# Where the first x tiles are transposed, and on which queue w1's first pieces travel: a silu MLP on one core

## The chip, the cores and the metric

One core of a Trainium2 chip runs the whole program. The time is device microseconds of one execution; the time before is the median of three runs.

## The reference

```python
# x: 1 x 2048 x 640, w1: 640 x 1728, w2: 1728 x 640, all bf16
h = jnp.einsum("bsd,df->bsf", x, w1)
h = jax.nn.silu(h)
out = jnp.einsum("bsf,fd->bsd", h, w2)
```

## The kernel before, in words

The 2048 rows of x are four row chunks of 512 (`sc` 0 to 3). The contraction of the first product, 640, is five tiles of 128 (`dt` 0 to 4). The 1728 columns of w1 are thirteen column tiles of 128 (`ft` 0 to 12) and a tail of 64.

TensorE needs x transposed, with the contraction on the partitions: `xT_sb[:, dt, rows]`. For chunks 1 to 3 all five tiles come by DMA transpose, straight from x in memory (`transpose_x`, L152, on SP's queue). For chunk 0 the tiles come in two ways: tiles 0 to 2 are loaded as they lie (`load_x0`, L144, into `x0_sb`), transposed on TensorE by four 128x128 transposes each (`transpose_x0`, L181, against an identity), and copied from PSUM to `xT_sb` by VectorE (tiles 0 and 2, L185) or ScalarE (tile 1, L187); tiles 3 and 4 come by one DMA transpose each.

w1's columns 0 to 767 (column tiles 0 to 5) come as one load of 192 KB for each contraction tile (`w1_0` to `w1_4`, L148), the rest in two loads for all five contraction tiles: `w1_a` (column tiles 6 to 9, 640 KB) and `w1_b` (column tiles 10 to 12 and the tail, 560 KB).

TensorE's order is written by hand. After a few matmuls on constants (L171) and the transposes of tile 0, `column_group` (L262) computes column tiles 0 to 5 of chunk 0 at once in six PSUM banks: the outer loop is over the contraction tiles, the inner one over the six column tiles, so each contraction tile is used for six matmuls as soon as it is there. After the second matmul of tile `dt` it calls `transpose_next(dt + 1)`, which puts the transposes of the next tile into TensorE's stream if that tile is transposed there, and otherwise only notes the DMA to wait for. The first matmul of tile `dt` waits for that x tile and for `w1_dt`. Then `unit` (L220) computes column tiles 6 to 12 of chunk 0, each with five matmuls; the first of them waits for `w1_a`. Chunk 1 has a `column_group` and units again, chunks 2 and 3 have units alone, and two `tail_unit`s (L230) compute the last 64 columns of two chunks each. A column tile's silu is a sigmoid on ScalarE (L204) and a product on VectorE (L207).

The second product (L325) follows, with copies out of PSUM (L336, L338) and the stores.

SP issues, in this order: half of x's tile 0, `w1_0`, `w1_1`, `w1_2`, the transpose of tile 3, `w1_4`, the transpose of tile 4, `w1_a`, `w1_b`, then the fifteen transposes of chunks 1 to 3 (the first of which wait for `w1_a`), with w2's loads after ten of them. ScalarE issues: the other half of tile 0, tile 1 (`x0_c`), tile 2 (`x0_d`), `w1_3`; then comes its activation table load and a small activation (L162), and only then its copy of tile 1. Waits are semaphore waits that `Plan` puts ahead of an instruction for the operations it depends on.

Of the kernel before, what the change touches and what calls it, by code (L numbers as in the profile page):

```python
# [20 lines left out]
class Plan:  # L21
# [9 lines left out]
    def add(self, eng, emit, deps=(), group=None):  # L31
        op = Op(eng, emit, [d for d in deps if d is not None], group)
        self.ops.append(op)
        return op
# [40 lines left out]
def bass_standalone__dense_activation_silu__prompt_kernel(  # L75
# [9 lines left out]
    xf = x.flatten_outer_dims()  # L85
# [3 lines left out]
    P = 128  # L89
    H = P // 2  # L90
    SCH = 512
    DT = D // P
# [5 lines left out]
    JB = SCH // P  # L98
# [4 lines left out]
    with ExitStack() as es:  # L103
        def sb(name, shape, dtype):
            return es.enter_context(nc.sbuf_tensor(name, shape, dtype))

        xT_sb = sb("xT_sb", [P, DT, S], bf16)
# [18 lines left out]
        bank_free = [[] for _ in range(NBANK)]  # L126
        turn = [0]

        def take_bank():
# [5 lines left out]
        FA = 6  # L135
        w1_cuts = [FA, 10, FT]
        id_a = add("pool", lambda e: e.memset(ident[:, :], 0.0))
        id_b = add("pool", lambda e: e.affine_select(
            out=ident[:, :], in_=ident[:, :], compare_op=ALU.not_equal, fill=1.0,
            base=0, pattern=[[-1, P]], channel_multiplier=1), [id_a])  # L140
        warm = add("dve", lambda e: e.memset(warm_sb[:, :], 0.0))

        def load_x0(eng, name, j0, j1, d0, d1):
            return add(eng, lambda e: e.dma_start(  # L144
                out=x0_sb[:, j0:j1, d0 * P:d1 * P], in_=x0_v[:, j0:j1, d0 * P:d1 * P]), group=name)

        def load_w1(eng, name, d0, d1, f0, f1, deps=()):
            return add(eng, lambda e: e.dma_start(  # L148
                out=w1_sb[:, d0:d1, f0:f1], in_=w1_v[:, d0:d1, f0:f1]), deps, group=name)

        def transpose_x(sc, dt, name, deps=()):
            return add("sp", lambda e: e.dma_start_transpose(  # L152
                out=xT_sb[:, dt, sc * SCH:(sc + 1) * SCH],
                in_=xf[sc * SCH:(sc + 1) * SCH, dt * P:(dt + 1) * P]), deps, group=name)

        x0_a = [load_x0("sp", "x0_a", 0, JB // 2, 0, 1), load_x0("act", "x0_b", JB // 2, JB, 0, 1)]
        w1_lo = [load_w1("sp", "w1_0", 0, 1, 0, FA * P)]
        x0_c = [load_x0("act", "x0_c", 0, JB, 1, 2), load_x0("act", "x0_d", 0, JB, 2, 3)]
        w1_lo += [load_w1("sp", f"w1_{dt}", dt, dt + 1, 0, FA * P) for dt in (1, 2)]
        x0_t = {3: transpose_x(0, 3, "x0_3")}  # L160
        w1_lo += [load_w1("act", "w1_3", 3, 4, 0, FA * P), load_w1("sp", "w1_4", 4, DT, 0, FA * P)]
        add("act", lambda e: e.activation(out=warm_sb[:, :], in_=warm_sb[:, :], func=ACT.Sigmoid), [warm])  # L162
        x0_t[4] = transpose_x(0, 4, "x0_4")
        w1_dma = [load_w1("sp", f"w1_{name}", 0, DT, w1_cuts[g] * P, min(w1_cuts[g + 1] * P, F))
                  for g, name in enumerate("ab")]

# [9 lines left out]
        def transpose_x0(dt, j0, j1, b):  # L176

            dst = ps[:, b, :].bitcast(bf16)[:, j0 * P:j1 * P]
            out = xT_sb[:, dt, j0 * P:j1 * P]
            for j in range(j0, j1):  # L180
                t = add("pe", lambda e, j=j: e.transpose(  # L181
                    dst[:, (j - j0) * P:(j - j0 + 1) * P], x0_sb[:, j, dt * P:(dt + 1) * P], ident[:, :]),
                    [x0_a[j // (JB // 2)], id_b] if dt == 0 else [x0_c[min(dt, 3) - 1]] + bank_free[b])
            if dt % 2 == 0:
                c = add("dve", lambda e: e.tensor_copy(out=out, in_=dst), [t])  # L185
            else:
                c = add("act", lambda e: e.copy(out=out, in_=dst), [t])  # L187
            bank_free[b] = [c]
            return c
# [49 lines left out]
        x_dma, x1_of, w2_dma = {}, [], []  # L239
        for sc in range(1, NSC):  # L240
            for dt in range(DT):
                x_dma[sc] = transpose_x(sc, dt, f"x1_{dt}" if sc == 1 else f"x{sc}", [w1_dma[-2]])
                if sc == 1:
                    x1_of.append(x_dma[sc])
            if sc == 2:
                half = FR // 2
                for a, z in ((0, half), (half, FR)):
                    w2_dma.append(add("sp", lambda e, a=a, z=z: e.dma_start(
                        out=w2_sb[:, a:z, :], in_=w2_v[:, a:z, :]), group="w2"))
                for hh in range(2):  # L250
                    w2_dma.append(add("sp", lambda e, hh=hh: e.dma_start(
                        out=w2_sb[hh * H:(hh + 1) * H, FR, :], in_=w2[FR * P:F, :]), group="w2"))
# [18 lines left out]
        def transpose_next(dt):  # L271
            if dt in x0_t:
                x0T.append(x0_t[dt])
            elif dt < DT:
                x0T.append(transpose_x0(dt, 0, JB, FA + dt % 2))

        half = [transpose_x0(0, k * JB // 2, (k + 1) * JB // 2, FA - 2 + k) for k in range(2)]
        x0T = [half[1]]
        warm_up([SCH, 2 * P])
# [121 lines left out]
```

## Time and profile before

| | us |
|---|---|
| median of three runs (lowest to highest) | 125.83 (125.35 to 126.18) |
| the profiled execution's own time | 126.35 |
| its span, first to last instruction | 124.9 |

The early transfers, with the time at which the issue starts and, by the view of DMA issues, the time from there to landing:

| transfer | KB | queue | issue starts, us | to landing, us |
|---|---|---|---|---|
| x tile 0, two halves | 64 each | SP, ScalarE | 0.73, 0.74 | 2.1, 2.3 |
| `w1_0` | 192 | SP | 1.25 | 2.8 |
| `x0_c` | 128 | ScalarE | 1.26 | 3.2 |
| `w1_1` | 192 | SP | 1.75 | 3.4 |
| `x0_d` | 128 | ScalarE | 1.79 | 4.3 |
| `w1_2` | 192 | SP | 2.21 | 4.5 |
| `w1_3` | 192 | ScalarE | 2.35 | 4.5 |
| transpose of tile 3 | 128 | SP | 2.69 | 4.6 |
| `w1_4` | 192 | SP | 3.94 | 4.0 |
| transpose of tile 4 | 128 | SP | 4.55 | 3.7 |
| `w1_a` | 640 | SP | 5.73 | 6.4 |
| `w1_b` | 560 | SP | 6.35 | 7.2 |

How to read the profile: PE is TensorE's matmul, PEld its weight load, which overlaps the matmul before it; DVE is VectorE, ACT ScalarE; SPq and ACTq are instructions by which SP and ScalarE issue DMAs. `w_sb` stands for the tiles of w1 and w2, `x_sb` for `x0_sb`, and L152 is line 152 of the kernel. In the chain of waits each piece is the work that ended last, in order of time. All transfers of one queue go to the same 16 DMA engines; a transfer has landed when the last of them is done.

### The profile page before, as it was taken

Reading aid. Unit: us, or ns where it says so; the run is one execution under the profiler, and the core shown is the slowest. Engines: PE = TensorE matmul, PEld = TensorE weight load, DVE = VectorE, ACT = ScalarE, POOL = GpSimd, SP = SyncE. Lnnn points to the kernel's source line nnn. Section 1 sums busy time; section 2 is a strip of 40 time slices with the busy share of each in tenths; the row PEclk is TensorE's granted clock in tenths of the full one; section 3 lists DMA queues with packets and bytes.
Section 4 is the critical chain, followed back from the end, with each engine's and each line's share of the span. In section 5 each row is a group of like instructions: output and inputs, shape, how many; then the busy total and the mean of one; then the engine's idle time right before and its main releaser. Section 6 shows DMA issues by size and latency. Waiting matters only on the chain.

```text
span 124.9 us, 2083 instructions
## 1 busy us (share of the span) xinstructions
PE 121.9 (98%) x894; PEld 57.2 (46%) x894; DVE 45.2 (36%) x71; ACT 38.9 (31%) x68; POOL 0.7 (1%) x6
## 2 busy tenths in 40 slices
PE   7999999999999999999999999999999999999992
PEld 2444444444444444444444444444444444445482
DVE  0111985069666666666673020202020120202022
ACT  0503953087555555555540010101010110101021
POOL 2000000000000000000000000000000000000000
PEclk9999999999999999999999999999999999999999
DMA  3996384559980000000000001114120201112434
GB/s 86 314 273 239 90 89 98 113 132 381 306 170 0 0 5 0 3 0 0 0 0 5 0 0 32 26 21 154 66 105 5 105 0 21 26 21 74 157 104 111
DMA packets 20185, 10.41 MB, mean 83 GB/s; under 512 B 14416, under 2 KB 20176, under 8 KB 20176
## 3 DMA queue, kind: packets, MB, share of 16 engines
q1 hardware_dynamic: 18416, 9.62, 28.8%
q10 hardware_dynamic: 1760, 0.66, 2.0%
q8 instruction: 7, 0.11, 0.4%
q14 instruction: 2, 0.02, 0.1%
HBM read 4.90 MB, written 2.62 MB: 60 GB/s over the span
## 4 chain that ended last, share of the span: by engine, by line
PE 98%; DVE 0%; issue 0%
PE ps L325 47%; PE ps L220 35%; PE ps L262 11%; PE ps L171 3%; PE ps L230 2%; PE ps L181 1%; DVE o_sb L336 0%
## 5 line engine op out<-in xcount | busy, mean ns | idle before, releaser
L325 PE MATMUL ps<-w_sb,hT_sb 64*128 64x512 bf16 (+2 forms) x486 | 47.3, 352 | 0.0
L207 DVE TENSOR_TENSOR hT_sb<-ps,sig_sb 128x512 bf16<-128x512 f32 (+1 forms) x56 | 37.1, 688 | 21.6 <-ACT sig_sb L204 21.5
L220 PE MATMUL ps<-xT_sb,w_sb 128*128 128x512 bf16 x200 | 43.5, 379 | 0.0
L204 ACT ACTIVATE sig_sb<-ps 128x512 bf16<-128x512 f32 x54 | 30.7, 605 | 27.9 <-PE ps L220 16.4
L325 PEld LDWEIGHTS ps<-w_sb,hT_sb 64*128 64x128 bf16 x486 | 23.5, 94 | 23.5
L220 PEld LDWEIGHTS ps<-xT_sb,w_sb 128*128 128x128 bf16 x200 | 19.5, 98 | 23.7 <-DMA w_sb<-in_w_dram 0.3
L336 DVE CAST o_sb<-ps 128x512 bf16<-128x512 f32 (+2 forms) x9 | 5.7, 632 | 37.6 <-PE ps L325 37.6
L338 ACT CAST o_sb<-ps 128x512 bf16<-128x512 f32 (+2 forms) x9 | 4.8, 539 | 38.5 <-PE ps L325 38.5
L262 PE MATMUL ps<-xT_sb,w_sb 128*128 128x512 bf16 x60 | 14.5, 395 | 0.0
L325 PE MATMUL ps<-hT_sb,w_sb 64*128 64x512 bf16 x108 | 12.3, 376 | 0.0
L262 PEld LDWEIGHTS ps<-xT_sb,w_sb 128*128 128x128 bf16 x60 | 5.9, 101 | 7.2 <-issue 0.5
L325 PEld LDWEIGHTS ps<-hT_sb,w_sb 64*128 64x128 bf16 x108 | 5.2, 94 | 6.5 <-issue 0.4
L336 DVE CAST oT_sb<-ps 128x512 bf16<-128x512 f32 x2 | 1.4, 692 | 11.7 <-PE ps L325 11.7
L338 ACT CAST oT_sb<-ps 128x512 bf16<-128x512 f32 x2 | 1.2, 587 | 13.6 <-PE ps L325 13.6
L171 PE MATMUL ps<-const-bfloat16-1.0 128*128 128x512 bf16 (+1 forms) x8 | 3.3, 572 | 0.8 <-PEq L386 0.8
L185 DVE COPY xT_sb<-ps 128x256 bf16<-128x256 bf16 (+1 forms) x3 | 0.9, 336 | 6.2 <-PE ps L181 6.2
L230 PE MATMUL ps<-xT_sb,w_sb 128*64 128x512 bf16 x20 | 2.3, 381 | 0.0
L162 ACT ACT_TABLE_LOAD x1 | 1.3, 1283 | 2.9 <-issue 2.9
L171 PEld LDWEIGHTS ps<-const-bfloat16-1.0 128*128 128x128 bf16 x8 | 1.0, 137 | 1.9 <-issue 1.9
L181 PEld LDWEIGHTS ps<-ident,x_sb 128*128 128x128 bf16 x12 | 1.3, 129 | 1.2 <-DMA x_sb<-in_x_dram 0.6
L181 PE MATMUL ps<-ident,x_sb 128*128 128x128 bf16 x12 | 1.7, 281 | 0.0
L230 PEld LDWEIGHTS ps<-xT_sb,w_sb 128*64 128x64 bf16 x20 | 1.0, 110 | 1.2 <-issue 0.4
(9 smaller groups left out, 1.8 us busy)
## 6 DMA issues: line engine op xcount, KB each, us to landing
out_dram<-o_sb SPq DMA_DIRECT2D x14, 160.0 KB, 1.9
w_sb<-in_w_dram SPq DMA_DIRECT2D x1, 1120.0 KB, 7.7
w_sb<-in_w_dram SPq DMA_DIRECT2D x1, 960.0 KB, 5.6
w_sb<-in_w_dram SPq DMA_DIRECT2D x4, 192.0 KB, 3.7
w_sb<-in_w_dram SPq DMA_DIRECT2D x1, 640.0 KB, 6.4
w_sb<-in_w_dram SPq DMA_DIRECT2D x1, 560.0 KB, 7.2
xT_sb<-in_x_dram SPq DMA_TRANSPOSE x17, 3.1
x_sb<-in_x_dram ACTq DMA_DIRECT2D x2, 128.0 KB, 3.7
```

The source lines that it names most:

```text
L162: add("act", lambda e: e.activation(out=warm_sb[:, :], in_=warm_sb[:, :], func=ACT.Sigmoid), [warm])
L171: add("pe", lambda e, n=n: e.matmul(ps[:, NBANK - 1, 0:n], lhsT=ones[:, 0:P], rhs=ones[:, 0:n], start=True, stop=True))
L181: t = add("pe", lambda e, j=j: e.transpose(dst[:, (j - j0) * P:(j - j0 + 1) * P], x0_sb[:, j, dt * P:(dt + 1) * P], ident[:, :]), [x0_a[j ...
L185: c = add("dve", lambda e: e.tensor_copy(out=out, in_=dst), [t])
L204: a = add("act", lambda e: e.activation(out=sig_sb[:, s, 0:n], in_=ps[:, b, 0:n], func=ACT.Sigmoid), [pe, sig_free[s]])
L207: v = add("dve", lambda e, rows=rows, ft=ft, cols=cols: e.tensor_tensor(out=hT_sb[rows, ft, cols], in0=ps[rows, b, 0:n], in1=sig_sb[rows, ...
L220: pe = add("pe", lambda e, dt=dt: e.matmul(ps[:, b, 0:n], lhsT=w1_sb[:, dt, ft * P:(ft + 1) * P], rhs=xT_sb[:, dt, cols], start=(dt == 0), ...
L230: pe = add("pe", lambda e, dt=dt, hh=hh: e.matmul(ps[hh * H:(hh + 1) * H, b, :], lhsT=w1_sb[:, dt, FR * P:F], rhs=xT_sb[:, dt, (sc + hh) * ...
L262: pe = add("pe", lambda e, dt=dt, ft=ft: e.matmul(ps[:, banks[ft], :], lhsT=w1_sb[:, dt, ft * P:(ft + 1) * P], rhs=xT_sb[:, dt, sc * SCH:( ...
L325: pe = add("pe", lambda e, b=b, n=n, lhsT=lhsT, rhs=rhs, ft=ft: e.matmul(ps[:, b, 0:n], lhsT=lhsT, rhs=rhs, start=(swap == 0 and ft == 0), ...
L336: ev = add("dve", lambda e, b=b, n=n, dst=dst: e.tensor_copy(out=dst, in_=ps[:, b, 0:n]), [pe])
L338: ev = add("act", lambda e, b=b, n=n, dst=dst: e.copy(out=dst, in_=ps[:, b, 0:n]), [pe])
```

## The change

x's tile 2 of chunk 0 is no longer loaded and transposed on TensorE, but comes by DMA transpose, and tiles 3 and 4 come in one DMA transpose of 256 columns. `w1_2`, `w1_3` and `w1_4` are issued by ScalarE. SP's order becomes: half of tile 0, `w1_0`, `w1_1`, the transpose of tile 2, the transpose of tiles 3 and 4, `w1_a`, `w1_b`, and the rest as before. ScalarE's becomes: half of tile 0, `x0_c`, `w1_2`, `w1_3`, `w1_4`, and then the table load. TensorE's stream loses the four transposes of tile 2, and VectorE's their copy. `transpose_x` takes ranges of rows and tiles; for chunks 1 to 3 it moves what it moved.

```diff
-        def transpose_x(sc, dt, name, deps=()):
+        def transpose_x(name, r0, r1, d0, d1, deps=()):
             return add("sp", lambda e: e.dma_start_transpose(
-                out=xT_sb[:, dt, sc * SCH:(sc + 1) * SCH],
-                in_=xf[sc * SCH:(sc + 1) * SCH, dt * P:(dt + 1) * P]), deps, group=name)
+                out=xT_sb[:, d0:d1, r0:r1], in_=xf[r0:r1, d0 * P:d1 * P]), deps, group=name)
...
-        x0_c = [load_x0("act", "x0_c", 0, JB, 1, 2), load_x0("act", "x0_d", 0, JB, 2, 3)]
-        w1_lo += [load_w1("sp", f"w1_{dt}", dt, dt + 1, 0, FA * P) for dt in (1, 2)]
-        x0_t = {3: transpose_x(0, 3, "x0_3")}
-        w1_lo += [load_w1("act", "w1_3", 3, 4, 0, FA * P), load_w1("sp", "w1_4", 4, DT, 0, FA * P)]
+        x0_c = load_x0("act", "x0_c", 0, JB, 1, 2)
+        w1_lo += [load_w1(("sp", "act")[dt > 1], f"w1_{dt}", dt, dt + 1, 0, FA * P) for dt in range(1, DT)]
         add("act", lambda e: e.activation(out=warm_sb[:, :], in_=warm_sb[:, :], func=ACT.Sigmoid), [warm])
-        x0_t[4] = transpose_x(0, 4, "x0_4")
+        x0_t = {2: transpose_x("x0_t2", 0, SCH, 2, 3), 3: transpose_x("x0_t3", 0, SCH, 3, DT)}
+        x0_t[4] = x0_t[3]
...
-                    [x0_a[j // (JB // 2)], id_b] if dt == 0 else [x0_c[min(dt, 3) - 1]] + bank_free[b])
+                    [x0_a[j // (JB // 2)], id_b] if dt == 0 else [x0_c] + bank_free[b])
...
-                x_dma[sc] = transpose_x(sc, dt, f"x1_{dt}" if sc == 1 else f"x{sc}", [w1_dma[-2]])
+                x_dma[sc] = transpose_x(
+                    f"x1_{dt}" if sc == 1 else f"x{sc}", sc * SCH, (sc + 1) * SCH, dt, dt + 1, [w1_dma[-2]])
```

## Prediction

> **What bounds the kernel now.** I read the page first: who is busy, and which chain ends last.
>
> ```profile
> PE 121.9 (98%) x894; PEld 57.2 (46%) x894; DVE 45.2 (36%) x71; ACT 38.9 (31%) x68; POOL 0.7 (1%) x6
> ...
> PE 98%; DVE 0%; issue 0%
> PE ps L325 47%; PE ps L220 35%; PE ps L262 11%; PE ps L171 3%; PE ps L230 2%; PE ps L181 1%; DVE o_sb L336 0%
> ```
>
> TensorE is the whole chain. So an edit of the opening can win only the TensorE work it takes out, and can lose whatever time it makes TensorE wait. Next the chain of waits in order of time (start, duration, what):
>
> ```profile
> 5.66 1.68 PE ps L262 x6
> 7.34 0.22 PE ps L181 x4
> 7.56 4.75 PE ps L262 x22
> 12.31 7.56 PE ps L220 x35
> ```
>
> The second row is the four transposes of tile 2, the only TensorE work that the change removes: 0.22 us. Matmuls go at 4.75 / 22 = 0.216 us each. Then TensorE's weight loads, with what ended the idle time before them, and SP's rows of the same stretch:
>
> ```profile
> 12.11 1.12 SPq L152 DMA_TRANSPOSE xT_sb<-in_x_dram  x1
> 12.14 0.33 PEld L220 LDWEIGHTS ps<-xT_sb,w_sb 128*128 128x128 bf16 x3 [0.32 <-DMA w_sb<-in_w_dram]
> ```
>
> The first matmul of column tile 6 starts exactly when w1_a lands (SP's transpose, which waits for the same load, starts at 12.11). Nearly no TensorE time is lost there, but nothing is in hand either. Last, the DMA side: busy time by stretch (the last two numbers are the 16 engines' share and GB/s), and the transfers of a late stretch:
>
> ```profile
> 6.30:8.30 2.00, 2.00 (x14) 1.05 (x13) 0.42 (x1) 0.00 (x0) 0.00 (x0) 1.00 1.06 230
> 8.30:10.20 1.90, 1.90 (x10) 0.85 (x9) 0.00 (x0) 0.00 (x0) 0.00 (x0) 1.00 1.02 355
> ```
>
> ```profile
> DMA packets 39, 0.03 MB, mean 23 GB/s; under 512 B 0, under 2 KB 39, under 8 KB 39
> ## 3 DMA queue, kind: packets, MB, share of 16 engines
> q1 hardware_dynamic: 39, 0.03, 6.7%
> ```
>
> The engines are full to 10.2 us. From 8.3 to 10.2 they move 1.9 x 355 = 675 KB, about all of w1_a (640 KB), which nevertheless lands at 5.73 + 6.4 = 12.1. The second view (11.8 to 13.3) says why: a share of 6.7% is one engine of sixteen, still working alone. One engine lags, and w1_a and w1_b land with it. I read w1_a as 10.5 without that lag (10.2, and some 0.3 from last packet to landing), so the lag is 1.6 us.
>
> **The change, part by part.** TensorE loses four transposes: -0.22 us from 7.18 on. VectorE's copy of tile 2 (0.42 us) goes too; VectorE then idles 3.9 us, so that is worth nothing. The 22 matmuls start at 7.18 in place of 7.40, so the needs become: tile 2 at 8.04, tile 3 at 9.34, tile 4 at 10.63, column tile 6 at 11.93.
>
> ScalarE's queue: x0_d goes, w1_2 and w1_4 come, one issue of 0.53 us more. The table load goes from 2.91 to 3.44 and the warm activation ends at 4.96 in place of 4.43. What is queued behind is the copy of tile 1, which starts at 5.70 when TensorE delivers: 0.74 us of cover, price nothing; if an issue took over 1.3 us, tile 1 would be late by the excess.
>
> SP's queue: after w1_1 comes tile 2's transpose at 2.21, issue 1.13 to 1.26 us by the undisturbed rows, 1.20 for the row in the same place; then the double one at 3.46. No row shows a double transpose. Low bound: one issue, 1.2, so w1_a goes out at 4.7 against 5.73. Middle: two singles, 2.4, w1_a at 5.9. High: twice the longest row (1.93, behind w2's loads), 3.9, w1_a at 7.4. I take between the first two, since the rows of the loaded opening are 1.13 and 1.20.
>
> DMA work: x0_d is 512 pieces of 256 bytes, a transposed tile moves the same bytes. A steady transpose costs 0.45 of the engines for its 1.3 us step, 0.59 us; the DMA records give 18 ns a piece for x0_d too, 512 x 18 / 16 = 0.58. So the swap is neutral. Bytes ahead of w1_a are unchanged, and the engines stay full, since ScalarE's three 192 KB loads are queued by 3.5 us. All of it should be done where it is done today: the last tile lands at 4.55 + 3.7 = 8.3 now.
>
> When each lands: the two queues seem to share the engines about evenly from 4 us. w1_1 (0.53 us of work, a quarter already done) is through at 4.8, tile 2 at 5.9, landing at 6.6 with 0.7 for the tail (tile 3 today: pieces done near 6.6, landed 2.69 + 4.6 = 7.3). w1_2 at 5.6, w1_3 at 6.8, w1_4 at 7.6; the double one at 8.4 to 8.9. Cover: tile 2 1.4 us, w1_2 2.4, w1_3 2.5, w1_4 3.0, tiles 3 and 4 0.4 to 0.9 (tile 3 has 2.2 today). The thin one is the double transpose: tile 3 now waits for both halves.
>
> A transpose of four 128x128 blocks lands 2.6 us after its issue when alone, and the next one follows in 1.3 us, so blocks overlap. The Trainium skill (VectorE: DVE Perf Modes, The three transpose paths) gives one 128x128 transpose 390 ns on TensorE and 1309 ns by DMA, which speaks against the swap; by that, an estimate, twelve DMA blocks in a row would end near 17.9. The trace does not agree: four blocks in 2.6 us are half of that, and they overlap. What the rule would mean here is rival E.
>
> w1_a: same bytes ahead, same lag: 12.1, bounds 10.5 (no lag) and 13.8 (lag once more, or issued 1.6 later). TensorE wants it at 11.93. At 12.1 the 0.22 that was saved is spent waiting. w1_b (13.6 against a need of 16.5) and the first tile of the next rows (14.7 against 19.9) are far from being next.
>
> Sum: -0.22, given back up to 0.2: 0 to -0.22, I take -0.05. Against the profiled execution of 126.35 (span 124.9, 1.4 around it) that is 126.3; the median of the runs is 0.5 lower, so the forecast is 125.83 - 0.05 = 125.8.
>
> **The rivals.**
> B, slower: the double transpose is dear behind a loaded queue. For: transposes behind loads took up to 7.5 us to land and 1.93 to issue (the w2 stretch), and no row shows a double. At 3.46 + 7.5 = 10.9 tile 3 is 1.6 late, net +1.4; at 3.9 of issue w1_a goes out 1.63 later and lands at 13.7, net +1.6. The two overlap. Price 126.1 to 127.6, as one number 127.4. It decides where the double lands after 9.56 (9.34 + 0.22), and passes 1% at 10.8. Against: the opening's rows took 4.6 and 3.7 behind similar loads.
> C, slower: the lagging engine lags a second 1.6 us in w1_a, because ScalarE's queue is still on the engines when w1_a starts: 127.4. Against: w1_4 should be through before.
> E, slower: DMA transposes do not overlap, each starting when the one before has landed. From rows, three tiles at 2.6 us: 2.21 + 7.8 = 10.0 against 9.34, net +0.45, 126.3. The Trainium skill's figure has this form, with the dearer block. Against: the steps of 1.3 us.
> D, faster: w1_a, issued up to 1 us sooner and behind fewer transfers on its own queue, escapes the lag and lands near 10.5. Then the whole 0.22 stays: 125.6; and executions in which TensorE is ahead of the profiled one (125.35 was seen) would no longer be held at w1_a, down to some 124.9, or a little less. Against: the lag's cause is not visible, so nothing says it moves.
> That the transposes stay on TensorE is excluded: the changed program has 28 matmuls in a row after the four transposes of tile 1.
>
> **How the numbers follow.** A, the forecast, 0.45: runs spread from 0.48 under to 0.35 over their median, so 125.1 to 126.2. B 0.30, C 0.09, D 0.14, E 0.02. What a measurement here can tell from no change is about 1%, 1.26 us. Slower by that: B's upper part 0.23, C 0.08, A 0.02, together 0.33. Faster by that: half of D, 0.07, since 0.30 us is all that TensorE's stream of this execution has (0.22 and the 0.08 between the warm-up and w1_0). Same 0.60. The range runs from A's low end, 125.1, to 127.6, B's high end; 0.06 of D lies below, C's tail and the dearest of B, 0.1, above.
>
> **What the changed profile would show.** Right: one chain row of 28 matmuls of column_group with no transposes in it; its end near 12.1; TensorE's weight load of column tile 6 waiting 0.3 to 0.5 us for w1; the double transpose issued in 1.2 to 2.4 us and landed by 9.3. B: a wait of TensorE for xT_sb near 9.3, or SP issuing w1_a after 6.5. C: w1_a landing after 13 with w1_a issued before 6. D: no wait at column tile 6, w1_a landed before 11.5. I would be wrong altogether if TensorE waited before 8 us (w1_1, tile 1's copy, tile 2), which I gave over half a microsecond of cover each.

## The result, and the profile after

The changed kernel takes 127.02 us (median of six, 126.06 to 127.15), the kernel before 125.68 beside it (125.32 to 126.18): a ratio of 1.0101 (1.0064 to 1.0138), 1.3 us slower. The forecast was 125.8, with a chance of 0.60 that no change could be told.

The profiled execution of the changed kernel is its fastest: 126.06, span 124.7. Even so its page shows the new wait. Shares of the span by engine and by line of the chain, then TensorE's weight loads of the column group (busy, mean ns, idle before, and what ended most of it):

```profile
PE 92%; DMA 5%; SPq 1%; issue 0%; DVE 0%
PE ps L325 47%; PE ps L219 34%; PE ps L262 8%; DMA xT_sb<-in_x_dram 5%; PE ps L229 2%; SPq L148 1%; SPq L144 0%; DVE o_sb L336 0%
...
L262 PEld LDWEIGHTS ps<-xT_sb,w_sb 128*128 128x128 bf16 x60 | 5.6, 98 | 8.0 <-DMA xT_sb<-in_x_dram 1.1
```

TensorE was 98% of the chain; now a DMA transpose has 5%. The chain of waits in order of time names it:

```profile
2.22 5.78 DMA xT_sb<-in_x_dram
8.00 0.05 issue
8.04 4.08 PE ps L262 x18
```

That is tile 2: issued at 2.22, landed at 8.00, where 6.6 was forecast. TensorE has nothing left to do for tile 1 and stands until it lands, 0.4 us in this profile; the group's last 18 matmuls (tiles 2 to 4) follow. Another 0.3 us went before: the first matmul of tile 1 starts at 6.33, just behind the landing of `w1_1`. The transfers, from the trace, against the forecast: `w1_1` landed at 6.2 (its data were to be through at 4.8), `w1_4` at 8.4 (7.6), the double transpose at 9.3 (8.4 to 8.9), `w1_a` at 11.1 (12.1). The DMA engines by stretch (the last two numbers of a row are their share and GB/s), of the changed kernel, then of the kernel before:

```profile
4.20:6.30 2.10, 2.02 (x11) 0.75 (x9) 0.00 (x0) 1.42 (x3) 0.00 (x0) 1.00 1.03 239
6.30:8.30 2.00, 1.71 (x8) 0.66 (x9) 0.00 (x0) 0.00 (x0) 0.00 (x0) 1.00 1.18 230
```

```profile
4.20:6.30 2.10, 2.10 (x9) 1.01 (x9) 0.00 (x0) 0.81 (x2) 0.00 (x0) 1.00 1.13 333
```

The engines are busy all the time, share 1.03 and 1.18, and yet move 239 GB/s from 4.2 to 6.3, where the same stretch of the kernel before has 333. They are full of work that goes slowly. (From 6.3 to 8.3 both of these profiles have 230.)

The two profiles on record are a poor pair: by their spans the changed kernel is 0.2 us faster. TensorE's matmul step goes from 0.427 to 0.216 us at a time that moves from execution to execution: 6.3 us in the first profile of the kernel before, 4.9 in the one of the changed kernel. So second profiles of both came first among the experiments.

### The profile page after: what moved, and what is told of

It reads as the page before. It is cut to its first block, busy times and chain, and to the rows that moved or that the text cites. A ratio compares the mean times of both kernels' runs of the same rounds, so it can differ in the third digit from the quotient of the medians.

```text
span 124.7 us, 2067 instructions
## 1 busy us (share of the span) xinstructions
PE 121.1 (97%) x885; PEld 56.3 (45%) x890; DVE 44.7 (36%) x70; ACT 38.8 (31%) x68; POOL 0.7 (1%) x6
## 4 chain that ended last, share of the span: by engine, by line
PE 92%; DMA 5%; SPq 1%; issue 0%; DVE 0%
PE ps L325 47%; PE ps L219 34%; PE ps L262 8%; DMA xT_sb<-in_x_dram 5%; PE ps L229 2%; SPq L148 1%; SPq L144 0%; DVE o_sb L336 0%
## 5 line engine op out<-in xcount | busy, mean ns | idle before, releaser
L219 PE MATMUL ps<-xT_sb,w_sb 128*128 128x512 bf16 x196 | 43.3, 379 | 0.2
L262 PE MATMUL ps<-xT_sb,w_sb 128*128 128x512 bf16 x59 | 14.1, 387 | 0.4 <-DMA xT_sb<-in_x_dram 0.3
L184 DVE COPY xT_sb<-ps 128x256 bf16<-128x256 bf16 x2 | 0.5, 292 | 2.6 <-PE ps L180 2.6
L180 PEld LDWEIGHTS ps<-ident,x_sb 128*128 128x128 bf16 x8 | 0.8, 123 | 1.0 <-DMA x_sb<-in_x_dram 0.7
L180 PE MATMUL ps<-ident,x_sb 128*128 128x128 bf16 x8 | 1.0, 265 | 0.0
```

The lines of the kernel that those rows point to most:

```text
L180: t = add("pe", lambda e, j=j: e.transpose(dst[:, (j - j0) * P:(j - j0 + 1) * P], x0_sb[:, j, dt * P:(dt + 1) * P], ident[:, :]), [x0_a[j ...
L219: pe = add("pe", lambda e, dt=dt: e.matmul(ps[:, b, 0:n], lhsT=w1_sb[:, dt, ft * P:(ft + 1) * P], rhs=xT_sb[:, dt, cols], start=(dt == 0), ...
L262: pe = add("pe", lambda e, dt=dt, ft=ft: e.matmul(ps[:, banks[ft], :], lhsT=w1_sb[:, dt, ft * P:(ft + 1) * P], rhs=xT_sb[:, dt, sc * SCH:( ...
```

## The experiments

Each is compared with the kernel before, run beside it on the same chip. "The rate" is GB/s from 5.0 to 7.5 us, where the changed kernel's transposes and w1 loads meet. A diff is against the changed kernel, or against the kernel before where the text says so; `...` marks what is left out of it. The letters A to D in the expectations of e1 to e4 name theories of these experiments, not the rivals of the prediction, which has the same letters.

**e1, the changed kernel again, unaltered.**

> The changed kernel once more, unaltered, for a second profile, because the profiled execution took 126.06 and the six others 126.99 to 127.30 or so. Theory A (the two queues share the engines, so x's tiles 2 to 4 come late): tile 2 lands at 8.0 to 9, the double transpose at 9.3 to 10.5, TensorE waits for xT_sb once or twice, and the landing of the last of them sets the time: 127.0 with a double transpose some 1 us later than the 9.32 seen. Theory B (one DMA engine lags): one of the transfers lands 1 us or more after the others of its age, with a stretch in which the engines' share is about 0.06. Theory C (TensorE's clock): same landings as in the first profile, but the matmuls go at 0.427 us until after 6.3 us.

126.91, ratio 1.0066 (1.0038 to 1.0094), so the loss is 0.8 us here and 1.3 in the first comparison, with intervals that overlap. Its profile is of an execution of 127.07. The chain of waits:

```profile
2.22 6.71 DMA xT_sb<-in_x_dram
8.93 0.05 issue
8.98 4.06 PE ps L262 x18
```

Tile 2 at 8.93, the double transpose at 9.7, in theory A's windows, though it was tile 2 and not the double transpose that set the time; no transfer came a microsecond after its fellows, and the fast matmul step was there by 4.3 us, so neither B nor C. TensorE had issued its last matmul of tile 1 at 6.89 and the next at 8.98: less one step of 0.22, it stood for 1.9 us. The rate is 165.

**e2, the kernel before again.**

> The kernel before, unaltered, for a second profile: all theories 125.7. A: no wait of TensorE for xT_sb; tile 4 lands near 8.3. B: w1_a again near 12.1 with one engine alone at the end. C: the time at which the matmul step goes from 0.427 to 0.216 moves between profiles (6.3 in the first).

125.84, ratio 1.0000 (0.9973 to 1.0027). Its profile has the fast step by 4.2 us and span 124.2:

```profile
1.25 3.63 DMA x_sb<-in_x_dram
...
6.62 0.22 PE ps L181 x4
6.84 4.75 PE ps L262 x22
11.59 2.59 PE ps L220 x12
```

The column group ends at 11.59, in e1 at 8.98 + 4.06 = 13.04: 1.45 us apart, and the spans are 124.2 and 125.6, 1.4 apart. So the whole difference of these two profiles stands ahead of the group's end, where e1 has its wait of 1.9 us for tile 2; nothing behind it gives or takes. `w1_a` landed at 10.6 here, with no engine alone at the end: the lag of the first profile is not in every execution. TensorE's only wait on the chain is tile 1 (landed 4.88).

**e3, the transposes alone**: w1's early loads on the queues of before.

```diff
-        w1_lo += [load_w1(("sp", "act")[dt > 1], ...) for dt in range(1, DT)]
-        x0_t = {2: transpose_x("x0_t2", 0, SCH, 2, 3), 3: transpose_x("x0_t3", 0, SCH, 3, DT)}
+        w1_lo += [load_w1("sp", ...) for dt in (1, 2)]
+        x0_t = {2: transpose_x("x0_t2", 0, SCH, 2, 3)}
+        w1_lo += [load_w1("act", "w1_3", ...), load_w1("sp", "w1_4", ...)]
+        x0_t[3] = transpose_x("x0_t3", 0, SCH, 3, DT)
```

> The changed transposes with w1's loads on the queues of before. A: the order in one queue is that of before, tile 2 behind w1_2, so w1_1 lands near 5.1 and w1_4 near 8; the transposes still land by 8.5 to 9, a small wait at most: 125.4 to 126.0. If it is the transposes themselves (rival D: a double transpose is dear), the double one lands after 9.6 here too and the time stays at 126.6 to 127.1. B: near 126 to 127, as the lag falls.

125.81, ratio 0.9998 (0.9969 to 1.0026): level. Tile 2 landed at 6.9, the double transpose at 8.5, rate 281. The chain goes through `w1_a` instead:

```profile
5.86 5.59 DMA w_sb<-in_w_dram
11.45 0.05 issue
11.49 2.55 PE ps L221 x11
```

TensorE was through with the group 0.4 us before `w1_a` landed. So the four transposes taken off TensorE do end in a wait for `w1_a`, as forecast, and transposes as such, the double one too, cost nothing here.

**e4, the queue alone**: the kernel before with `w1_2` and `w1_4` issued by ScalarE.

```diff
-        w1_lo += [load_w1("sp", f"w1_{dt}", ...) for dt in (1, 2)]
-        w1_lo += [load_w1("act", "w1_3", ...), load_w1("sp", "w1_4", ...)]
+        w1_lo += [load_w1(("sp", "act")[dt > 1], f"w1_{dt}", ...) for dt in range(1, DT)]
```

> The kernel before with w1_2 and w1_4 moved to ScalarE's queue and nothing else. A: w1_1 no longer late, since x0_d with its small pieces stands ahead of w1_2 on ScalarE's queue, but w1_2 comes later, at 7 to 8, and tile 3 is not hurt: 125.5 to 126.3. D: 125.7, since the transposes are single. B and C: 125.7.

126.36, ratio 1.0033 (1.0006 to 1.0060). Within 0.1 of A's time, but not its picture: tile 3's transpose, said to be unhurt, was issued at 2.21 and landed at 9.1, 6.9 us later, where it took 4.6 before; tile 4 took 7.1 where it took 3.7. The rate is 181. No tile 2 and no double transpose is involved: single transposes beside ScalarE's loads are enough. In this profile TensorE did not wait for them, since tiles 3 and 4 are used last; it waited 0.1 us for `w1_2`, which landed at 8.1. Where the 0.4 us of the median comes from it does not show. One candidate that was not tested is ScalarE's longer issue: its warm-up activation ends at 5.72 here, and only then can it copy tile 1, a copy that starts at 5.36 in e2.

**e5, the double transpose split** into one for tile 3 and one for tile 4.

```diff
-        x0_t = {2: ..., 3: transpose_x("x0_t3", 0, SCH, 3, DT)}
-        x0_t[4] = x0_t[3]
+        x0_t = {2: ..., 3: transpose_x("x0_t3", 0, SCH, 3, 4)}
+        x0_t[4] = transpose_x("x0_t4", 0, SCH, 4, DT)
```

> The changed kernel with tiles 3 and 4 in two DMA transposes again. Mixing theory (DMA transposes on one queue and large copies on the other, in flight together, slow both): tile 2 still lands at 8 to 9, some 6 us after its issue, and as it sets the time nothing is won: 126.6 to 127.2. Rival (the double transpose is the dear part): tile 3 comes earlier, 126.0 or less.

127.10, ratio 1.0106 (1.0069 to 1.0143): as slow. Tile 2 landed at 8.7, rate 211. The double transpose, the prediction's rival B, is out as the cause.

**e6, tile 2 as a plain load** in the transpose's place on SP's queue, transposed on TensorE.

```diff
+        x0_c.append(load_x0("sp", "x0_d", 0, JB, 2, 3))
-        x0_t = {2: transpose_x("x0_t2", 0, SCH, 2, 3), 3: transpose_x("x0_t3", 0, SCH, 3, DT)}
+        x0_t = {3: transpose_x("x0_t3", 0, SCH, 3, DT)}
```

> The changed kernel, but tile 2 is loaded as it lies, on SP's queue in the transpose's place, and transposed on TensorE as before. The same bytes at the same place in the same queue beside the same three loads. Mixing theory: the plain load lands by 5.5 to 6.5, the three w1 loads are almost through before the double transpose moves, the double lands by 8.4 to 9.2, time 125.6 to 126.2. Rival (fair sharing only: SP's queue comes late because ScalarE's takes half): the plain load lands at 8 to 9 like the transpose, and the time stays near 126.9.

126.42, ratio 1.0068 (1.0028 to 1.0107); the load landed at 6.9, 0.4 outside the forecast and 1.1 to 2.0 before the transpose in the same place; the double one, which still met the rest of the copies, at 9.1. The rate is 263. The executions scatter from 125.8 to 127.7. By the landing it speaks for mixing; the time, 0.2 over the forecast, settles nothing.

**e7, one queue**: all five early w1 loads on SP's queue, in the order `w1_0`, `w1_1`, `w1_2`, tile 2, `w1_3`, `w1_4`, tiles 3 and 4.

> The changed transposes with all five of w1's early loads on SP's queue, w1_3 too, so that no large copy on ScalarE's queue can meet a transpose. Mixing theory: tile 2 lands by 6.5, the double transpose by 8.5, TensorE waits at most for w1_a: 125.4 to 125.9. Rival (fair sharing): the same order of bytes, the same time, and no gain over the kernel with w1_3 on ScalarE (125.8). Lag of one engine: 126 or more in the executions where it falls on a tile.

126.27, ratio 1.0024 (1.0002 to 1.0046), 0.4 over the forecast. The tiles were early (6.3; 8.8 for the double, 0.3 late), so the transposes are in time again at a rate of 261, but tile 1 landed at 5.0 and TensorE waited for it. A little slower than e3, for which I have no tested reason.

**e9, the cost by itself**: the kernel before, with w2's first 960 KB issued by ScalarE while chunk 1's transposes run.

```diff
-                for a, z in ((0, half), (half, FR)):
+                for a, z in ((half, FR),):
...
         column_group(0, x0T, w1_lo, transpose_next)
+        w2_dma.append(add("act", lambda e: e.dma_start(
+            out=w2_sb[:, 0:FR // 2, :], in_=w2_v[:, 0:FR // 2, :]), group="w2a"))
```

> The disputed cost by itself, away from the opening: the kernel before with the first 960 KB of w2 issued by ScalarE after chunk 0's first column group, beside the steady transposes of chunk 1, which had steps of 1.3 us and landed after 2.6 to 2.8. Mixing theory: the transposes beside it land after 4 to 7 us and the two together move 100 to 200 GB/s, less than the 350 that copies alone move; the time is 125.7 to 126.3, since chunk 1 has 5 us in hand. Rival (fair sharing): transposes need 0.45 of the engines and the copy takes the rest, the total over 250 GB/s, landings of 3 to 4 us.

The clearest of all, by its rate. The second transpose of chunk 1 was issued 0.3 us before the copy; in the profile of before the first two of chunk 1 land after 2.6 and 2.8 us. Here, DMA issues first, then three stretches:

```profile
xT_sb<-in_x_dram SPq DMA_TRANSPOSE x1, 8.6
```

```profile
13.40:15.40 2.00, 2.00 (x11) 0.94 (x10) 2.00 (x5) 1.54 (x3) 0.00 (x0) 1.00 0.75 105
16.00:17.40 1.40, 1.40 (x8) 0.64 (x7) 1.04 (x2) 0.91 (x2) 0.00 (x0) 1.00 1.04 389
19.00:20.40 1.40, 1.22 (x6) 0.37 (x4) 0.89 (x2) 0.55 (x1) 0.00 (x0) 1.00 1.90 35
```

And what moved in the first of them, by queue (q1 is SP's, q10 ScalarE's):

```profile
q10 hardware_dynamic: 63, 0.08, 47.0%
q1 hardware_dynamic: 508, 0.13, 27.8%
```

From 13.4 to 15.4 both queues are at work and together move 105 GB/s, no more than the transposes alone in the kernel before (101 to 103 in steps of 1.3 us) and less than a third of what the copy moves alone from 16.0 to 17.4, 389. 63 pieces of the copy hold 47% of 16 engines for 2 us, 239 ns each, while SP's transposes are being served beside them; from 16.0 to 17.4 a piece takes 55 ns (425 pieces, 104%). Fair sharing, which had over 250 in total, is refuted by this rate.

The copy lands at 18.8, the transpose, begun before it, at 20.6, later than even the mixing theory had it (4 to 7 us). But not all of that delay is the copy's. From 19.0 to 20.4, with the copy landed, the engines are full and move 35 GB/s, and the kernel before has such a stretch without any copy beside its transposes:

```profile
17.60:19.00 1.40, 1.40 (x8) 0.64 (x7) 1.01 (x2) 0.77 (x2) 0.00 (x0) 1.00 1.30 73
```

There its third and fourth transposes of chunk 1 land after 4.6 and 4.0 us. In both profiles one 16 KB transfer of the instruction queue starts shortly before the stretch, at 18.7 and at 17.4; that it is the cause is not shown.

The time of e9, 125.45, ratio 0.9972 (0.9941 to 1.0003), is under the forecast and shows no loss: chunk 1 had the time in hand but for a wait of 0.4 us.

**e10 and e12, no transposes in the opening**: the changed kernel's queues, order and bytes, but tiles 2 to 4 as plain loads on SP's queue, transposed on TensorE; run twice.

```diff
-        x0_t = {2: transpose_x("x0_t2", 0, SCH, 2, 3), 3: transpose_x("x0_t3", 0, SCH, 3, DT)}
-        x0_t[4] = x0_t[3]
+        x0_c += [load_x0("sp", "x0_d", 0, JB, 2, 3), load_x0("sp", "x0_e", 0, JB, 3, 4),
+                 load_x0("sp", "x0_f", 0, JB, 4, DT)]
+        x0_t = {}
```

> The changed kernel's queues, order and bytes, but tiles 2 to 4 are three plain loads on SP's queue in the transposes' place and are transposed on TensorE (12 more of its transposes than the changed kernel, 0.67 us at 0.056 each). Mixing theory: from 4.2 to 8.3 us the engines move 310 to 380 GB/s in place of 200 to 240, the last of tiles 2 to 4 and w1_2 to w1_4 lands by 8.0, w1_a by 10.2 without a lag; time 125.8 to 126.4. Rival (sharing alone): the last x tile lands at 9 or later as with transposes, and the time is 127 or more.

> The kernel without transposes in the opening once more, unaltered, for a second profile. If one lagging engine made its tiles late, the lag shows again as a tail of few pieces on SP's queue, or it does not and tile 2 lands by 7.0; time 127 to 128 if it is there in most executions. The engines' rate from 5 to 7.5 us stays near 300 GB/s in both cases.

The rate holds: 300 and 305 GB/s, against 165, 211 and 225 in the three profiles with transposes there (e1, e5, the changed kernel's first). Rows for 5.0 to 7.5 us, of e1 and of e12:

```profile
5.00:7.50 2.50, 2.27 (x13) 0.76 (x9) 0.00 (x0) 0.64 (x2) 0.00 (x0) 1.00 1.10 165
```

```profile
5.00:7.50 2.50, 2.27 (x16) 0.98 (x15) 0.00 (x1) 0.59 (x1) 0.00 (x0) 1.00 1.11 305
```

Engines equally full, half the bytes. But the landings were a miss in e10: tiles 2 to 4 at 8.5, 9.3 and 9.7, the last forecast by 8.0, with a thin tail of pieces to 13 us as of one engine that is behind; in e12 at 7.0, 8.2 and 8.6. So plain loads can come late as well, at a full rate; whether the engine that is behind at the end made these late the views do not show. The times, 128.05 (ratio 1.0143, 1.0078 to 1.0207) and 126.83 (1.0075, 1.0038 to 1.0112), are over the forecast of 126.4. For that the order of TensorE's stream is a reason: the transposes of tile 2 stand ahead of the last four matmuls of tile 1, so a plain load is needed by TensorE that much sooner than a transposed tile. I compare landings and rates across the two kinds, not times.

**e11 and e13, `w1_2` back on SP's queue ahead of the x tiles**: e11 is the changed kernel so altered, e13 is e10 so altered.

```diff
-        w1_lo += [load_w1(("sp", "act")[dt > 1], ...) for dt in range(1, DT)]
+        w1_lo += [load_w1(("sp", "act")[dt > 2], ...) for dt in range(1, DT)]
```

> The changed kernel with w1_2 back on SP's queue ahead of the transposes, so that two copies, not three, are beside them. Mixing theory: the loss shrinks with the copies beside, tile 2 lands at 7.5 to 8.3, time 126.0 to 126.7, between 125.8 (one beside) and 126.9 (three). Rival (what counts is the place in SP's queue): tile 2, now one load further back, lands later than 8.9 and the time is 127 or more.

> The same with w1_2 back on SP's queue ahead of the x tiles, as was done to the kernel with transposes (126.9 to 125.9 there). Mixing theory: plain loads do not mind what is beside them, so moving one load changes little: tile 2 lands a little later, time within 0.4 of the kernel it is made from. Rival (number of copies on ScalarE's queue, whatever the other queue carries): it is rescued as well, by 0.7 us or more.

e11: 125.91, ratio 1.0001 (0.9971 to 1.0031), 0.1 under the forecast. One load moved, and the whole loss is gone. Its chain of waits:

```profile
2.69 5.06 DMA xT_sb<-in_x_dram
7.75 0.05 issue
7.80 4.06 PE ps L262 x18
```

Tile 2 stands one load further back in its queue, is issued 0.47 us later, and lands at 7.75, sooner than the 8.0 and 8.9 of the changed kernel and the 8.7 of e5. A place in a queue can't do that. By the time it moves, less is left of ScalarE's two loads (they landed at 6.1 and 7.3); the rate is 278. e13, the same move with plain loads: 127.42, ratio 1.0144 (1.0102 to 1.0186), tile 2 at 7.7, between e12's 7.0 and e10's 8.5, rate 305. The time lies 0.6 from either of its two parents' medians, over one and under the other, more than the 0.4 foretold; but it is not rescued. So the loss that e11 cures needs the transposes.

**Four attempts to beat both**, with `w1_a` cut in two loads (column tiles 6 and 7, then 8 and 9): f1 is e3 with the cut, f2 the kernel before with it, f3 is e9 with it, f4 is f1 with tile 1 in two halves on both queues.

```diff
-        w1_cuts = [FA, 10, FT]
+        w1_cuts = [FA, 8, 10, FT]
```

> The changed transposes on before's queues (the kernel that came out level at 125.8), with w1_a cut in two loads of 320 KB, column tiles 6 and 7 first. If w1_a is what bounds once the transposes are off TensorE and in time, its first half lands 0.9 us sooner and the wait of 0.4 us at column tile 6 goes: 125.3 to 125.5. If something earlier bounds (tile 1's load, the double transpose), 125.7 to 125.9.

> The kernel before with the same cut of w1_a. If w1_a with its lagging engine holds the executions in which TensorE is early: 125.4 to 125.7. If not, 125.8 to 125.9, no difference.

> The kernel before with w2's first 960 KB on ScalarE's queue (125.45 against 125.89 in three rounds, interval up to 1.0003) and the cut of w1_a. If that gain was real, 125.1 to 125.5; if it was scatter, 125.6 to 126.1, with TensorE waiting some 0.4 us for chunk 1's second tile at 20 us, as it did there.

> The first of these with x's tile 1 in two halves, one on each queue, ahead of w1_1. Tile 1 landed at 4.25 to 5.25 in the profiles so far and TensorE waited for it in three of them. If that wait is on the path, 125.1 to 125.4; if w1_1, 0.15 us later, or w1_a is what binds, as the first of these.

Ratios: f1 0.9990 (0.9967 to 1.0012), f2 0.9983 (0.9959 to 1.0008), f3 0.9994 (0.9967 to 1.0021), f4 1.0000 (0.9977 to 1.0022). All level with the kernel before. The cut did take `w1_a` off the path in the profile of f1 (first half landed at 9.4), and the chain then goes through tile 1's load, 4.98; f4's halves did not mend that, its SP half landed at 5.5. e9's small gain did not come back in f3. No version here beats the kernel before by more than the interval.

## Why the prediction was wrong

**The step that failed** is the one on DMA work: "So the swap is neutral. Bytes ahead of w1_a are unchanged, and the engines stay full", and "All of it should be done where it is done today". The pieces and bytes were right, the engines were full, and it still took longer: 165 to 225 GB/s from 5.0 to 7.5 us in three profiles (the changed kernel's two and e5), against 290 and 304 in two of the kernel before. I priced transposes from rows where they ran alone and copies from rows where they ran alone, and added. A transpose on SP's queue and a large copy on ScalarE's in flight together do not add; e9 shows the pair at the rate of the transposes alone, and e10 and e12 that the rate holds when no transpose is there. In e12 the plain loads even land where the adding up had put the transposes, within 0.4 us (7.0 for 6.6, then 8.2 and 8.6 for 8.4 to 8.9); in e10 they do not (8.5 to 9.7). In the kernel before the two hardly met: by the time its first transpose moved, ScalarE had one load left. The change put tile 2's transpose a load sooner and two more copies beside it, which e11 undoes with one load.

The landing times then fell with that step. Tile 2: forecast 6.6, measured 8.0, 8.7 (e5) and 8.9 (e1), 1.4 to 2.3 us late, the terms that were to add up to a wait of nothing. The prediction had named the sign, "wrong altogether if TensorE waited before 8 us", and two terms of it were at work: tile 2, and in the first profile `w1_1` with 0.3 us. That the measured 127.02 still lies in the stated range of 125.1 to 127.6 is luck: the range reaches so far for rival B, whose cause was not at work.

**The cover was taken from one execution.** "Tile 2 1.4 us" of cover counted from a need at 8.04, which holds where the fast matmul step begins at 6.3 us. In e1, e5 and the profile of after it began before 5, and TensorE was ready for tile 2 at 6.89 + 0.22 = 7.1, 7.3 and 7.6. So 0.4 to 0.9 us of the cover was not there. In e1 the wait of 1.9 us is made of both: tile 2 was needed 0.9 us before 8.04 and used 0.9 us after.

**TensorE's -0.22** was right as work: behind tile 1's transposes the group has matmuls alone, 10 up to the wait and 18 behind it, and in e3 it goes where the forecast had it go, into a wait for `w1_a` (e3's ratio is 0.9998). In the changed kernel `w1_a` was not what bound: it landed at 11.1 and 11.5 and TensorE was not ready for it. It was tile 2 that was next, a wait that I had set aside with "over half a microsecond of cover".

**The double transpose.** Its issue took 1.3 us (3.46 to 4.76), near the low bound of 1.2; the forecast had taken a value between 1.2 and 2.4. Rival B named the right outcome for the wrong thing: it priced a dear double "behind a loaded queue" at 127.4, but e5, without a double, is as slow, and e3, with one behind more loads of its own queue, is level. What counts here is not what lies ahead in its own queue but what runs beside it in the other.

**C and D.** C had "ScalarE's queue is still on the engines", which came true, but for the tiles, not for `w1_a`. D's landing of `w1_a` came near (11.1 for 10.5, no lag), without a gain, since tile 2 had been waited for already. ScalarE's longer issue (table load at 3.5, copy of tile 1 at 5.4 in the changed profile) cost nothing, as priced. E is out: in e1 the first two transposes of chunk 1, alone on the engines, landed 1.2 us apart (14.2 and 15.4), less than half of what one takes.

The Trainium skill (DMA: Bandwidth & Descriptors, Issuing engines are not separate DMA queues) says that DMAs of several issuing engines run on the same 16 engines and interleave, so that issuing from two saves only issue time. For plain copies this case agrees: 305 GB/s in e12 and in e13, with three loads and with two on ScalarE's queue. For transposes beside copies it does not go far enough: issuing from the second queue cost 0.8 to 1.3 us here. The Trainium skill (Advanced Engine Details and Errata, X-Bar Transpose (TRN2)) holds transposes to be as fast as regular DMAs. This case differs: alone, in the kernel before, they move 101 to 103 GB/s at a share of 0.45, one in 1.3 us, and beside the other queue's copy, e9 has the two at 105 GB/s together.

**Open.** How the two slow each other, inside the engines or at the writing side, no run shows. Nor why one engine lags in some executions (the first profile of before, e10) and not in others (e2), nor what the slow stretch is that transposes without a copy have in the kernel before from 17.6 to 19.0. Whether smaller pieces of the copy would mend it was not tried.

## What to carry to other kernels

Prices of transfers taken from stretches where each kind runs alone don't add when a DMA transpose of one queue meets large copies of another: look in the profile which of them will be in flight together, and read the rate, not the busy share, of that stretch. Keep copies that a transpose would meet on the transpose's own queue, or ahead of it; here one 192 KB load moved back (e11) was worth the whole loss, and all early loads on one queue (e7) brought the transposes back in time. And take the cover of a transfer from the earliest need that any execution shows, not from the one profile at hand.

## What the runs showed of the hardware that was not expected

The busy share of the DMA engines says nothing of this loss: 1.10 at 165 GB/s (e1) and 1.11 at 305 (e12). In e9, pieces of one copy took 239 ns each beside transposes (63 pieces, 47% of 16 engines, 2 us) and 55 ns without them (425 pieces, 104%, 1.4 us). The share even reads 1.90 where 35 GB/s move (e9, 19.0 to 20.4).

The time at which TensorE's matmul step halves moves by 2 us between executions of one kernel (6.3 us and by 4.2 in the two profiles of the kernel before). The column group ends 0.72 us apart there (12.31 and 11.59), which is the whole difference of the spans (124.9 and 124.2); how much of the scatter of 125.3 to 126.2 it is in other executions is not shown. It can turn the sign of a comparison of two single profiles, as it did in the pair on record.
